# One activation function for the second MoE's gate, named ring places, and another order of the work

## The chip, the cores and the metric

The kernel runs on one core of a Trainium2 chip. The metric is the device time of one execution in microseconds (us). The core has a matrix engine (TensorE, PE in the profile; its weight loads are PEld), three elementwise engines (VectorE is DVE, ScalarE is ACT, GpSimd is POOL) and a queue that issues DMA transfers (SyncE, SP). Each engine runs its own instructions in the order written, and waits on semaphores for the others.

## The reference

Attention of 4 batches and 8 heads (576 positions, 64 wide) with a threshold, then two MoE layers over the 2304 tokens it gives (512 wide, hidden 2048), all in fp32:

```python
scores = scale * q @ k.T
scores = where(scores >= max(scores) - tau, scores, -1e9)
attn = exp(scores - max(scores)); attn = attn / (sum(attn) + 1e-9)
x = (attn @ v)                       # heads side by side: 2304 x 512
h = x @ w1_in;  x = (h * clip(h + 3, 0, 6) / 6) @ w1_out
h = x @ w2_in;  x = (h * 1 / (1 + exp(-1.702 * h))) @ w2_out
```

## The kernel before, in words

**Precision.** An fp32 operand of a matmul is split into a high part and the low remainder, and each product is three matmuls (high by high, high by low, low by high). A split is a copy on ScalarE (the high part) and a subtraction on VectorE or GpSimd (the low part, `tt`, L494, so all of these stand under L495). Weights arrive in another number format and are decoded by two ScalarE, three VectorE and one GpSimd instruction each (`decode`, L521, tile `wmstg`), then split into rings of eight tiles (`inhring`, `inlring`, `outhring`, `outlring`).

**Stages.** From 0 to about 408 us the 16 pairs of heads are attended to (`unit`, L637): scores into the two `ps` banks of PSUM, a row maximum (L764), a threshold (L765), the exponential on ScalarE (L767), mask and sum (L768), normalising (L783 or L791), transposes by TensorE that are copied out of PSUM (`et`, L837 or L838), and the product with v (L910, L926). TensorE also does the first half of the first MoE in that time (`moe_a`, `gated`, L988 and L1013). To about 650 us the rest of the first MoE follows (`moe_b`, `wide`, L1103). From 650 us the second MoE runs in ten passes (`moe2`, L1252): two halves of the hidden width, each over four blocks of 512 tokens and one of 256. Half of its weights are decoded as these passes begin, kept in DRAM and fetched again.

**The second MoE's inner step.** `hidden2` (L1201) makes two hidden tiles from seven products in place of eight. Its partial sums go through ScalarE copies (`p`, `u`) and VectorE sums (`c`). `gate2` (L1188) then makes from each `c` the two operands `g` (high and low) of the output matmuls:

```python
add(ACT, ..., "RL",  activation(out=t, in_=c, func=Sigmoid, scale=1.702))   # L1195, tile tc
add(DVE, ..., "GT2", t = t * c)                                             # L1196, under L495
add(ACT, ..., "GH",  gh = copy(t))                                          # under L492
add(eng, ..., "GL",  gl = t - gh)                                           # under L495, eng POOL or DVE
```

There are 80 calls: 64 of 512 columns and 16 of 256. The output matmuls of a step (L1013, tile `py`) come after the hidden products of the next (L1214, tile `pm`).

**Places of tiles.** `buf` (L444) names a ring of tiles; all tiles of a ring share one tag of the pool, and the pool hands out the place that was given back first. In `Plan.link` (L184) the planner orders a tile's first use after all uses of the tiles one to two rings back.

**Order of the work.** Nothing is left to the framework: the functions above only add operations with a cost and a due time to a plan. `Plan.settle` (L337) takes two tables that stand in the file: `SWAPS`, the numbers of operations that run on their other engine (for instance a low part on VectorE rather than GpSimd), and `RANKS`, one priority for each of the 6046 operations. `Plan.order` (L212) then fills the engines by those priorities with modelled costs, keeping VectorE's and GpSimd's operations named in `PORT` from overlapping and at most eight transfers in flight. `Plan.fill` (L352) puts small matmuls on zeros and ones (L1379) where the plan leaves TensorE empty. The instructions are written in the order that comes out.

Of the kernel before, what the change touches and what calls it, by code (L numbers as in the profile page):

```python
# [1437 lines left out]
```

## Time and profile before

| | |
|---|---|
| time, median of 3 runs | 1052.87 us (1051.63 to 1053.76) |
| the profiled execution's own time | 1053.79 us |
| its span, first to last instruction | 1052.0 us |
| granted TensorE clock, mean | 0.999 |
| TensorE busy | 1032.8 us, 98% of the span |
| VectorE busy | 784.3 us, 75% |
| ScalarE busy | 609.6 us, 58% |
| GpSimd busy | 447.0 us, 42% |
| DMA | 150.09 MB, 143 GB/s in the mean |

The busy time of an engine is the union of its instructions. TensorE's instructions overlap: a matmul is shown from its entry to its modelled end, and the next one starts before that. So the pace of a run of matmuls is read from the time of the run over its count, and the idle time shown for TensorE is a little less than what a wait costs.

### The profile page before, as it was taken

Reading aid. Unit: us, or ns where it says so; the run is one execution under the profiler, and the core shown is the slowest. Engines: PE = TensorE matmul, PEld = TensorE weight load, DVE = VectorE, ACT = ScalarE, POOL = GpSimd, SP = SyncE. Lnnn points to the kernel's source line nnn. Section 1 sums busy time; section 2 is a strip of 40 time slices with the busy share of each in tenths; the row PEclk is TensorE's granted clock in tenths of the full one; section 3 lists DMA queues with packets and bytes.
Section 4 is the critical chain, followed back from the end, with each engine's and each line's share of the span. In section 5 each row is a group of like instructions: output and inputs, shape, how many; then the busy total and the mean of one; then the engine's idle time right before and its main releaser. Section 6 shows DMA issues by size and latency. Waiting matters only on the chain.

```text
span 1052.0 us, 19278 instructions
## 1 busy us (share of the span) xinstructions
PE 1032.8 (98%) x6962; PEld 931.5 (89%) x6962; DVE 784.3 (75%) x1642; ACT 609.6 (58%) x1208; POOL 447.0 (42%) x555
## 2 busy tenths in 40 slices
PE   8999899999999999999999999999999999999998
PEld 6677788798979888999999999899888988998988
DVE  7999899998989884778783356888787686465543
ACT  5897776666767775646443225665655565354433
POOL 5578778765867642555440116322331231000000
PEclk9999999999999999999999999999999999999999
DMA  8434465776867565346642314346463452321201
GB/s 228 123 107 139 138 184 170 200 196 185 244 205 199 179 200 158 110 147 210 208 139 78 95 56 138 104 149 195 136 203 108 145 173 59 101 81 41 88 33 51
DMA packets 86527, 150.09 MB, mean 143 GB/s; under 512 B 8480, under 2 KB 48032, under 8 KB 84384
## 3 DMA queue, kind: packets, MB, share of 16 engines
q1 hardware_dynamic: 86288, 148.57, 47.2%
q8 instruction: 55, 0.90, 0.4%
q14 instruction: 40, 0.33, 0.1%
q10 hardware_dynamic: 144, 0.29, 0.1%
HBM read 101.52 MB, written 47.32 MB: 141 GB/s over the span
## 4 chain that ended last, share of the span: by engine, by line
PE 81%; DVE 8%; ACT 3%; POOL 3%; issue 2%; DMA 2%; SPq 0%; DVEq 0%; ACTq 0%; POOLq 0%
PE py L1013 24%; PE pm L1214 14%; PE pm L988 10%; PE pm L1013 9%; PE pm L1103 7%; PE ps L708 5%; PE pm L926 4%; PE pm L834 4%; PE ps L748 1%; DVE g L495 1%; PE pm L910 1%; PE ps L732 1%; DVE outlring L495 1%; DMA wrawstg<-kept 1%; DVE e L768 1%
## 5 line engine op out<-in xcount | busy, mean ns | idle before, releaser
L1013 PE MATMUL py<-g,outhring 128*128 128x512 f32 (+3 forms) x1024 | 280.6, 358 | 2.4 <-DVE g L495 2.1
L1013 PEld LDWEIGHTS py<-g,outhring 128*128 128x128 f32 x1024 | 179.0, 188 | 21.0 <-DVE g L495 3.5
L1013 PE MATMUL py<-g,outlring 128*128 128x512 f32 (+3 forms) x512 | 182.8, 357 | 0.0
L1214 PE MATMUL pm<-outhring,inhring 128*128 128x256 f32 x512 | 145.0, 283 | 0.9 <-ACT u L492 0.4
L1214 PE MATMUL pm<-outlring,inhring 128*128 128x256 f32 x512 | 144.2, 282 | 0.9 <-DVE outlring L495 0.9
L1214 PE MATMUL pm<-outhring,inlring 128*128 128x256 f32 x512 | 143.8, 281 | 0.0
L764 DVE TENSOR_REDUCE nm<-ps 128x1 f32<-128x576 f32 x144 | 106.3, 750 | 15.6 <-PE ps L708 12.2
L767 ACT ACTIVATE e<-ps,nm 128x576 f32<-128x576 f32 x128 | 93.4, 739 | 38.9 <-DVE nm L764 33.4
L495 POOL TENSOR_TENSOR wmstg<-wmstg,wrstg 128x512 uint32<-128x512 uint32 x48 | 67.9, 1415 | 109.7 <-DVE wmstg L548 74.3
L495 POOL TENSOR_TENSOR g<-tc,g 128x512 fp32r<-128x512 f32 x24 | 33.2, 1384 | 185.1 <-ACT g L492 154.2
L768 DVE SCALAR_TENSOR_TENSOR e<-ps,th,e 128x576 f32<-128x576 f32 x128 | 102.7, 810 | 8.0 <-ACT e L767 6.0
L1013 PE MATMUL pm<-g,outhring 128*128 128x256 f32 (+1 forms) x512 | 106.5, 299 | 0.0
L495 POOL TENSOR_TENSOR g<-t,g 128x256 fp32r<-128x256 f32 (+2 forms) x68 | 61.4, 905 | 105.8 <-ACT g L492 91.0
L1013 PEld LDWEIGHTS py<-g,outlring 128*128 128x128 f32 x512 | 96.3, 188 | 11.1
L1214 PEld LDWEIGHTS pm<-outhring,inhring 128*128 128x128 f32 x512 | 96.6, 189 | 6.1 <-ACT u L492 1.6
L1214 PEld LDWEIGHTS pm<-outlring,inhring 128*128 128x128 f32 x512 | 96.8, 189 | 4.7 <-DVE outlring L495 1.6
L1214 PEld LDWEIGHTS pm<-outhring,inlring 128*128 128x128 f32 x512 | 97.3, 190 | 0.0
L988 PE MATMUL pm<-xh,inhring 128*128 128x256 f32 (+1 forms) x320 | 96.9, 303 | 0.2
L988 PE MATMUL pm<-xh,inlring 128*128 128x256 f32 (+1 forms) x320 | 94.5, 295 | 0.0
L988 PE MATMUL pm<-xl,inhring 128*128 128x256 f32 (+1 forms) x320 | 94.4, 295 | 0.0
L708 PE MATMUL ps<-kqv 128*128 128x288 f32 x480 | 81.5, 302 | 3.2 <-DVE e L768 1.5
L1013 PEld LDWEIGHTS pm<-g,outhring 128*128 128x128 f32 x512 | 82.3, 189 | 1.7 <-issue 1.4
(147 smaller groups left out, 2426.5 us busy)
## 6 DMA issues: line engine op xcount, KB each, us to landing
turned<-tr SPq DMA_DIRECT2D x16, 1024.0 KB, 3.9
et<-turned SPq DMA_DIRECT2D x64, 256.0 KB, 5.6
wrawstg<-in_w1i_dram SPq DMA_DIRECT2D x16, 512.0 KB, 4.0
wrawstg<-in_w1o_dram SPq DMA_DIRECT2D x16, 512.0 KB, 3.8
wrawstg<-in_w2i_dram SPq DMA_DIRECT2D x16, 512.0 KB, 4.0
wrawstg<-in_w2o_dram SPq DMA_DIRECT2D x16, 512.0 KB, 3.8
qk<-in_k_dram SPq DMA_DIRECT2D x24, 288.0 KB, 3.9
qk<-in_q_dram SPq DMA_DIRECT2D x24, 288.0 KB, 4.7
```

The source lines that it names most:

```text
L495: return lambda: (nc.vector if eng == DVE else nc.gpsimd).tensor_tensor(out=o(), in0=a(), in1=b(), op=op)
L708: nc.tensor.matmul(ps.t[:, i, :SH], q, w[hd].t[:, i * SH:(i + 1) * SH], start=a, stop=z)
L732: nc.tensor.matmul(ps.t[:, i, :SH], f32(qzb.t)[:, q0:q0 + P], f32(khb.t)[:, i * SH:(i + 1) * SH], start=True, stop=True)
L764: add(DVE, 672, K("R", s), "R", lambda: nc.vector.tensor_reduce(out=nm.t[:, c], in_=ps.t[:, :, :SH], op=ALU.max, axis=AX.XY, negate=True), ...
L767: add(ACT, 624, K("X", s), "X", lambda: nc.scalar.activation(out=ev(), in_=ps.t[:, :, :SH], func=ACTF.Exp, bias=nm.t[:, c]), [ps, (nm, s)] ...
L768: add(DVE, 736, K("M", s), "M", lambda: nc.vector.scalar_tensor_tensor(out=ev(), in0=ps.t[:, :, :SH], scalar=th.t[:, c], in1=ev(), op0=ALU ...
L834: nc.tensor.transpose(pt.t[:kn, o:o + P], src(), id_b.t)
L926: nc.tensor.matmul(pv[p].t[64 * hd:64 * hd + 64, :CH[p][1]], v_(k, hd), et_m(p, turned)[:, hd, k], start=k == 0, stop=False)
L988: nc.tensor.matmul(ph.t[:, :n], a, v, start=(cc == 0 and i == 0), stop=(cc == KC - 1 and i == 2))
L1013: nc.tensor.matmul(py.t[:, :n], a, v, start=(st and i == 0), stop=(sp and i == 2))
L1103: nc.tensor.matmul(ph.t[:, :n], a, v, start=(cc == 0 and q == 0), stop=(cc == KC - 1 and q == 2))
L1214: nc.tensor.matmul(o.t[:, :n], u.t[:, ws], v.t[:, xv], start=(st and kk == 0 and i == 0), stop=(sp and kk == 1 and i == 2), skip_group_che ...
```

## The change

Four things differ. `gate2` has one ScalarE instruction where it had a ScalarE and a VectorE instruction, so there are 80 operations fewer and all later operations have lower numbers. `buf` gives each place of a ring a tag of its own, so that a tile's place is its number modulo the ring's length. `RANKS` is another table (5966 numbers). `SWAPS` is another table: 294 entries in place of 291, of which 183 name the same operation as before.

```diff
 RANKS = """
-3IGWJhXH{B2mnO@LI55D)B$G!K>}?7@d20uivf`VkO5i&$N_x;bODY5<pGod!U1>zk^!IrxdG$>7XtSISOMt)vH_+6!2xptase&^#Q`h=90IHX^Z~U2(gFDa+yR6Em;pHg)&cqfqXFRo4g$sj?g97#u>m3iVglm<?Ey*xRs#M38v?Qdr2%vT
...
 SWAPS = (
-    22, 72, 185, 192, 212, 235, 236, 264, 269, 288, 309, 331, 340, 350, 360, 371, 393, 398, 486, 528, 542, 597, 630, 657, 659, 737, 738, 746, 803, 814, 846, 874, 880, 890, 892, 929,
...
+    22, 72, 113, 192, 212, 236, 247, 264, 269, 288, 309, 321, 331, 336, 340, 360, 371, 393, 486, 528, 542, 551, 597, 630, 657, 659, 667, 697, 713, 717, 719, 745, 814, 846, 874, 880,
...
@@ -442,7 +441,9 @@
     def buf(tag, ring, pool, shape, dt=F32):
-        return Buf(pl, tag, ring, lambda: pools[pool].tile(shape, dt, tag=tag, name=tag, bufs=ring), pool)
+        b = Buf(pl, tag, ring, None, pool)
+        b.make = lambda: pools[pool].tile(shape, dt, tag=f"{tag}{b.idx % ring}" if ring > 1 else tag, name=tag, bufs=1)
+        return b
@@ -1192,8 +1193,7 @@
-        add(ACT, act(T), K("RL2"), "RL", lambda: nc.scalar.activation(out=v(t)(), in_=v(c)(), func=ACTF.Sigmoid, scale=1.702), [c], [t])
-        add(DVE, dve(T), K("GT2"), "GT2", tt(DVE, v(t), v(t), v(c), ALU.mult), [c], [t])
+        add(ACT, act(T), K("RL2"), "RL", lambda: nc.scalar.activation(out=v(t)(), in_=v(c)(), func=ACTF.Gelu_apprx_sigmoid), [c], [t])
         add(ACT, 42 + act(T), K("GH2"), "GH", copy(v(gh), v(t)), [t], [gh])
```

The entries of `SWAPS`, counted with the operations they name: TensorE's copies `et` (L837) go to VectorE 23 times (18 before), remainders of the probabilities (`pk`, L783) 33 times (26 before), first-MoE high parts and remainders 13 and 23 times (15 and 27 before), the high parts of the first MoE's input (`xh`, L941) 4 times (11 before); the thresholds (L765) go to ScalarE 57 times (51 before). The number of VectorE operations in the plan goes from 1498 to 1405.

## Rows read from the trace of the kernel before

**Rows 1.** The page's first part: busy time, share of the span, instructions.

```profile
PE 1032.8 (98%) x6962; PEld 931.5 (89%) x6962; DVE 784.3 (75%) x1642; ACT 609.6 (58%) x1208; POOL 447.0 (42%) x555
```

**Rows 2.** Windows by stage: stretch, its length, engines' busy us, clock, DMA.

```profile
0.00:12.00 12.00, 9.83 (x45) 8.40 (x46) 6.54 (x20) 3.29 (x4) 5.71 (x24) 1.00 0.68 194
12.00:130.00 118.00, 111.83 (x791) 87.53 (x790) 111.25 (x265) 98.36 (x191) 82.94 (x103) 1.00 0.48 141
130.00:408.00 278.00, 274.54 (x2102) 240.95 (x2101) 243.54 (x587) 188.92 (x383) 180.89 (x295) 1.00 0.67 191
408.00:650.00 242.00, 241.62 (x1478) 235.23 (x1477) 156.98 (x301) 110.88 (x203) 95.47 (x77) 1.00 0.44 135
650.00:790.00 140.00, 136.64 (x898) 125.04 (x897) 113.09 (x200) 85.69 (x175) 45.46 (x32) 1.00 0.51 161
790.00:920.00 130.00, 129.75 (x820) 117.03 (x819) 87.61 (x155) 68.08 (x139) 27.48 (x19) 1.00 0.37 116
920.00:1052.00 132.00, 128.56 (x843) 117.31 (x841) 65.25 (x119) 54.38 (x116) 9.06 (x7) 1.00 0.18 59
```

**Rows 3.** The chain that ended last, its end: start us, us, what.

```profile
1039.82 9.00 PE py L1013 x75
...
1048.85 0.42 DVE yc L495
```

**Rows 4.** Waits of TensorE, 650 to 1052 us: total us, times, longest; longest two.

```profile
PE py L1013 <- DVE g L495: 1.8, 3, 0.9
PE pm L1214 <- DVE outlring L495: 0.9, 2, 0.7
```

**Rows 5.** Timeline around one such wait: start us, us, instruction, idle before.

```profile
710.50 0.42 DVE L495 TENSOR_TENSOR tc<-tc,c 128x256 f32<-128x256 f32 x1
710.84 1.50 DVE L495 TENSOR_TENSOR g<-tc,g 128x256 fp32r<-128x256 f32 x1
712.60 0.41 DVE L495 TENSOR_TENSOR g<-tc,g 128x256 fp32r<-128x256 f32 x1
...
710.72 1.34 POOL L495 TENSOR_TENSOR wmstg<-wmstg,wrstg 128x512 uint32<-128x512 uint32 x1 [16.56 <-ACT g L492]
...
712.40 0.38 PE L1013 MATMUL py<-g,outhring 128*128 128x256 f32 x1 [0.94 <-DVE g L495]
```

**Rows 6.** Groups of instructions, 650 to 1052 us: the gate's four, and L545.

```profile
L495 DVE TENSOR_TENSOR tc<-tc,c 128x512 f32<-128x512 f32 (+1 forms) x80 | 54.7, 686 | 26.2 <-ACT tc L1195 25.2
L1195 ACT ACTIVATE tc<-c 128x512 f32<-128x512 f32 (+1 forms) x80 | 46.8, 588 | 29.6 <-DVE c L495 26.2 <-DVE g L495 1.1 <-POOL g L495 1.1
L492 ACT ACTIVATE g<-tc 128x512 fp32r<-128x512 f32 (+1 forms) x80 | 46.4, 587 | 40.0 <-DVE tc L495 32.4 <-PE py L1013 7.4
L495 DVE TENSOR_TENSOR g<-tc,g 128x512 fp32r<-128x512 f32 (+1 forms) x56 | 39.9, 721 | 14.0 <-ACT g L492 11.2 <-PE py L1013 2.3
L545 ACT ACTIVATE wmstg<-wrawstg 128x512 f32<-128x512 f32 x18 | 11.9, 667 | 5.8 <-DMA kept<-wmstg 3.7 <-DVE wmstg L546 0.9 <-DVE inlring L495 0.6
```

**Rows 7.** Table loads of ScalarE among the groups of the whole span.

```profile
L767 ACT ACT_TABLE_LOAD x1 | 1.3, 1283 | 1.2 <-PEq L1426 1.2
L1195 ACT ACT_TABLE_LOAD x1 | 1.3, 1283 | 0.0
```

**Rows 8.** Waits of TensorE, 12 to 408 us: total us, times, longest.

```profile
PE pm L834 <- ACT et L837: 2.1, 5, 0.7
PE ps L708 <- DVE e L768: 1.5, 2, 0.8
PE pm L834 <- POOL er L783: 1.4, 1, 1.4
PE ps L708 <- DVE kqv L495: 1.1, 1, 1.1
```

**Rows 9.** Two groups of VectorE's instructions over the span.

```profile
L768 DVE SCALAR_TENSOR_TENSOR e<-ps,th,e 128x576 f32<-128x576 f32 x128 | 102.7, 810 | 8.0 <-ACT e L767 6.0 <-ACT th L766 0.3
L838 DVE COPY et<-pm 128x512 f32<-128x512 f32 (+1 forms) x18 | 10.9, 620 | 3.9 <-PE pm L834 2.7 <-DMA et<-turned 1.1
```

More of the change, by code (lines that the diff above doesn't have):

```diff
@@ L119 @@
[L119 to L120 removed]
+3IGWJ&H*g~2LMC>LjbG-9|E@lb^^NrQ38_!$pOj%?*W_v*8#=>+X1Qpn*z-N4g#nF;Q_1x?g3l^CIVvulL7Yu^8xY!1_HqWxdC7T9s;fcjRN}t6awu5AOZ>k>H)n0&jHc``~f%u=m8=EMFJ2400K<{GXgmRaso60YXV0CW&%V4X#!9J2LiVO
@@ new lines @@
+3j)~zuL6t$UILT?oC4Sa2m|#3Rsu)@=>nMo?*a(|5(An7ZURyQ+yd$X1OmhY&jMWn^a5uBR044Vr~=&rkpjO0^8#uDk^)ZxN&*D}3<HJ&Hv*~xC<C$rP6LAiWdipC;sP!M_5lq7egd)qzX7}fumO?*mjdGfKLb?*#R69XWCHO4p#h=+n*n42
+g8_>HjscGWP5}-9+5oWt*#NEpbOS~MqXQ!Y%>p+A<^p5`s{?5PN&zwfzycou-T=@5qyTpSQUERh4FHD%3jhQF6#>Ely#S^F6aWtZ004>rMgq105(1q9CjzDc3<4Pf-vI#t5&$It2ml2DApl|kRRFXALI45)5db^@3;+fI8~~{Rwg9yNUjQZm
+8Uic;%mS7Gr2(A)Fak{gcmlHkRRW0t{{f`}>j7;6%mFI`VFK&{?E+%~;{rzkQ~_@Ri2_IgIssMzF999_)dJ}Obpk#DB?2h|Dgu83F9HJqKLD%%Bmfft9{^hbl>n0fGXM|(Bmpr2{s8O%BLGVQ@BnH7=>Wa}odL@L7y?WI4+2>Me*w1uNdhhb
@@ new lines @@
+<O0|MIs&i)u>!gQdjcT>3IqB9KmytUbONIR9Rf@Od;-$}7Xq^ZngN~xsRGCXfdZcbhy!c_xB?Xd;sIj-(E#`W^#G0ltpGg%T>+>7b^w<E@c<eD8v(xnSpfS0WdXqevH(E=JOU5_76L*6{Q*A#HUbX;Jp%0jtOHsCz5!VRf&yLv0Rq$nYXran
+f&tV4+XB)7E&}HPo&o{_(E<4Z<pKTyfCAwHa{?g)h67sy6$5ty69Rz%i~!F7;{a~}c>ucrI01tINC0dAi2&CC*Z^w)C;*fIrvPdIGysnPBLbfQZUIFAlLLSNVF7*spaER~W&pSW2m-VL!vWy{PypWpwgf={DF7Y-iUD5%cmYcSSOQ`K%K`}j
+(*O$rDgm|vG6M?(D+3n;-~qY<ivltN`~p1#IRnQ6R09G7iUK+VA_EZvQUh574+AU%l>%A=Yy$uT8UsE9l>-<9Ujr=zGXuN>XagAo9Rqv=>jLBh&I4})mje?6M*~Fztpnl%WdoE0g9ESw=mIkY$pWGPJ^*V07yxz-bqa0@{sa93s0054D*?Iy
@@ new lines @@
+wE=Me-3mMl`3ma;vI8&#IRpU#>HsqVSq1P4#R~cgk^traV*||t@&g+LSOjbY5DQxh!3s(MjR4yK#{g*nIRJA2`~Y+SPXKiQhX95EH~=63Z~@Q(sR1nk1Oui53<dB3%K>i!H3IMgmjR>#F#;R|)d4~RECB-pQ322bg#rNsy8=oBGy_Bf4FlN%
+6az^Ecmv)7fCB^p{{XQ8?f~Eb#sCumc>zQL7XcChrvWqpB>|oQnE>km@&I@MnE}WFg#mH_b^#~?fB~lhBmz4EZ~|xoeF3uq#R1U*-2v_b`vM*V-vW{YU<29$&I0%W{Q|xN5(L)*2?I<3O8`3oQ2;#vF#ucu4FN^~Hvn1y5dmlbIsh902mxXN
+pa7)+dI2y2SOM<<PXV_BfdMK5^a1_?PyucONdc(?!vb6bUjhyTB?EH<K?6twAOn2^X9J)Dm;&kqUIbSIn*-<o)Bv9W)d0W%kN^q+`2fTL<NyN!^Z;7}<p5y-uK>6Jxd1x=ssLvJs{oh)!~nSi$N-`P9076#BLQLs3<10Xb^~Gq0|Z_JCjlG;
@@ new lines @@
+{{kumoddH2ngiAW!~@?1?gZ!qqyzT=A^}?g+yNs5$OGX6It11ODFnL%K?Jk|F9Zw(r37#Ungk&PyaZYV(FAG)p9B^J`2z3*O9XlZ*#t@iLj<q{cm!hvtpuS2cLccveFWJCqy$I=b_B!(f&@tfvIMaOaRiA3TLh{E1_kH@`UFG@U<9lL2nF~A
+g#_mW;{;&@zyn_d0R%P$!UVqro&*RB9SZ3R7X`HhKm`^BLIp$x$OJV74GT029t$xAI|V8Qcm>J@p9Pr(NClA#6$`!!Y6Xr3T?L2*(gl76rUlsrk_-F_QwwGT5dygakOHj&UIp<2@&d{NQvxpo`T_<6Z321%1q0^-s{$zl-~yoneFz!^asYk<
+H3Pi@uK^|j>;kj`j{;Kxa0BH7jsvj+4FuN%DFOHb76WJn9RY{{7y(=Xz5><&Km*DH+XL+bbpz=G-2>VKwgVUh2n50d3IrwuWdsxiSOXUX5(SV1g#da0eE@p^Dgc}SumIfv+yGPnG62N~#RJp=Z3E8(%mV@hf&*Ox!vjGAHUPc`c?5a``U5Zn
@@ L121 @@
++ZI3<C>Qn?M;8Yd;T8}VAr~7L85aZ>&lV~d;}#JY1{V$&#})w>`xeF)LKiI;_ZImU2^YN<I2Se-!xlpq?G`Z?GZ)wvN*6U3?iM2#AQwLu(H0mNFc&@-9v2!H)D}w@wiYxOI~V8{4;MujdluXl=@udv3KvNi
 """
 SWAPS = (
[10 rows of a table removed]
[10 rows of a table added]
 )
```

153 lines of the change are left out of this document (69 added, 84 removed), and 18 rows, old and new, of the table SWAPS.

## The prediction

> **What bounds the kernel now.** I read the page's busy times first, then the windows by stage, then TensorE's waits, and last the timeline around single waits. TensorE is busy for 1032.8 of 1052.0 us and no other engine for more than 784.3 [rows 1]. The windows [rows 2] show where it isn't: the difference of a stage's length and its PE busy time is 2.17 us at the start, 6.17 from 12 to 130 us, 3.46 to 408, 0.38 to 650, 3.36 to 790, 0.25 to 920 and 3.44 to the end, 19.23 in all. The clock column is 1.00 in every stage, so nothing is to be won there. The last matmuls run to 1048.82 and the last VectorE sum starts at 1048.85 [rows 3]; about 3.2 us of the 3.44 are that tail of sum and store, which the change leaves as it is. So about 14 us of idle time lie between start and tail, and no edit that leaves the matmuls alone can be worth much more. A little more, since idle time understates a wait: the last 75 matmuls pass at 9.00 / 75 = 0.12 us each [rows 3], but the one after a wait is shown for 0.38 us [rows 5]; about 0.2 us of an emptied pipe goes with each wait.
>
> The change touches the second MoE by its edit and the rest by its order alone, so the sum has one term for each.
>
> **The gate.** It removes 80 VectorE products of 0.686 us, 54.7 us in all [rows 6], a fifth of VectorE's 113.09 + 87.61 + 65.25 = 265.95 us in this stage [rows 2]. ScalarE keeps its 80 instructions of 0.588 us. The new function is in no row; its nearest rows are the copy of the same shape, 0.587 us, and another function at 0.667 us on wholly 512-wide tiles [rows 6], where the gate's mean holds 16 narrow ones. So it costs between nothing and 80 x 0.08 = 6.4 us of ScalarE, on an engine that is busy 208 of 402 us there [rows 2]; I take nothing, by the copy. Below nothing is excluded, as the copy does less and takes as long.
>
> Most of the 54.7 us was off the path. What was on it is seen in the waits: TensorE waited 1.8 us for the low parts `g` and 0.9 for the remainders `outlring` [rows 4], all of both made by VectorE. The timeline shows why they were late [rows 5]: a `g` of 256 columns that takes 0.41 us at its next place took 1.50, from 710.84, beside a GpSimd sum on weights from 710.72 for 1.34 us. TensorE's 0.94 us of idle time ends with it. So the waits come from VectorE and GpSimd being held up by one another in a moment that the order did not foresee. A product of the gate, 0.42 us, stood right ahead of it on VectorE, from 710.50 [rows 5]; without it the low part can start some 0.4 us sooner (0.69 where the tiles are 512 wide), before the GpSimd sum rather than behind it. What stays is the collision itself, with the roles changed.
>
> The Trainium skill, "SBUF — State Buffer", section on the two separate sides, says that a VectorE instruction with two SBUF inputs and a GpSimd instruction that reads SBUF exclude each other for a whole instruction, and whichever starts first holds the other up. The stretched `g` agrees: 1.34 us of GpSimd and then its own work. By that rule alone, with the moments of collision left to chance, taking out a fifth of VectorE's work there would take a fifth of these waits, some 0.7 us.
>
> I price the term from the idle time of 650 to 1048.8 us: 3.36 + 0.25 + (3.44 - 3.2) = 3.85, and about 8 waits with 0.2 us more each, 1.6; together 5.4 us are at stake. The lower end is all of it, -5.4. The upper end is that the same waits return once more behind other instructions, +3.8. I take -3.0: the 3.36 us of the first window, where VectorE is at 81% and where 0.4 to 0.7 us are taken from ahead of each late instruction, less a tenth. What would be late next is the partial sum `c` ahead of ScalarE, which waited 26.2 us for it already [rows 6]; it has slack, for TensorE has the products of the next step to do meanwhile.
>
> **The wait that is gone.** ScalarE sat idle for 40.0 us before the high parts, 32.4 of them until the product was there [rows 6]; afterwards two ScalarE instructions follow one another. Behind the new function on ScalarE stand the copies `p` and `u` out of PSUM, on which TensorE's next products hang. They move up, not back, as ScalarE has no longer to wait for VectorE between. I cost it at nothing beyond the term above; if the copies came later by one function, that is 0.588 us on one step, hidden by the other matmuls of the step, of which six alone last 0.7 us at 0.12 each.
>
> **Named places.** No instruction is added. A tile now waits for the tile one ring back and not for the place given back first. Rows of the nearest wait: the copy into `g` waited 7.4 us for TensorE to be done with a place [rows 6]. So it bounds the cost at +3 us, if half of that came onto the path, and at -1, if the pool's choice had been the worse one in the waits above. I take nothing, since the plan that makes the order already holds each tile back until the whole older ring is done. Transfers follow the same rule, and behind a held load on SP's queue would stand the loads of the next pass; the two longest waits of TensorE in this stage are none of that queue's [rows 4].
>
> **The order before 650 us.** Here instructions change places and engines, none goes. VectorE is at 111.25 of 118 us from 12 to 130 and 243.54 of 278 to 408 [rows 2], so the waits are those of a nearly full engine: 1.5 us for the masked probabilities, 2.1 for `et` from ScalarE, and single waits of 1.4 and 1.1 [rows 8]. `SWAPS` moves five more copies `et` (0.620 us each [rows 9]) and seven more remainders onto VectorE, and six thresholds, seven high parts and some weight parts away from it; my count leaves VectorE's load there the same within 1 us. So only the order can win or lose. The idle time at stake is 6.17 + 3.46 + 0.38 = 10.0 us, the lower end is half of it, -5, because the waits are ten or more of different kinds and a new order keeps some; the upper end is +7.3 (the second rival). I take -1.0: the two long single waits (1.4 and 1.1) are accidents of one place that another order does not repeat, and short ones replace them in part.
>
> **The sum.** -3.0 for the gate, -1.0 for the order, 0 for the rest: -4.0 against the profiled execution's 1053.79 (its span of 1052.0 and 1.8 around it). That execution was 0.92 us above the median of 1052.87; against the median the sum is 1048.9, which I state as 1049.0.
>
> **The rivals.**
>
> Nothing measurable (0.23). The collisions in the second MoE are those of weight work on GpSimd, which stays, and by the skill's rule above only a fifth of the waits goes. Then the gate wins about 0.7 us, the order nothing: 1052. For it: the sum is a quarter of one per cent of a kernel at 98% of TensorE. Against: the late low part stood right behind a product in VectorE's queue.
>
> Slower (0.16). Copies `et` move onto the engine that is already 94% busy from 12 to 130 us. There each of eight half units has a copy, 0.620 us, that can come in ahead of a mask and sum of 0.810 us, on which a score tile's place in PSUM hangs [rows 9]. Each mask that is late costs 0.81 us on TensorE. Four such (3.2 us) eat the gate's gain; from seven on (5.7 - 3.0 = 2.7) the kernel is measurably slower; nine give 7.3 - 3.0 = +4.3, 1057. For it: waits of this kind are there already, two of 0.8 at most [rows 8]. Against: six thresholds leave VectorE.
>
> A larger gain (0.15). The new order also takes half of the waits before 650 us: -5.4 - 5.0 = -10.4, 1042.5. For it: ten unlike waits, none of which is needed by the data alone. Against: a full VectorE.
>
> Table loads (0.03). If the copies and weight functions needed another table than the new function, ScalarE would load one at each change. Two loads of 1283 ns are all that the trace has, at the first exponential and at the first gate [rows 7]; the copies, and the function of L545, run on both sides of the second with no third. With one of them missing beside the new function, 80 gates need up to 160 loads, 205 us on an engine with 194 us to spare: 1100 or more. The skill's page "ScalarE: Activation LUTs", section on table sets, says that the cheap functions are in every set; hence so low a chance.
>
> **How the numbers follow.** My forecast, 1046 to 1050.7, has 0.43. What a measurement can tell from no change is 0.2%, 2.1 us: faster is below 1050.8, slower above 1055.0. Faster is 0.43 + 0.15 = 0.58, the same 0.23, slower 0.16 + 0.03 = 0.19. For 8 in 10 the range goes from the larger gain's 1042.5 to 1056.5 on the slower side, just short of its nine late masks.
>
> **What would show it.** After the change, VectorE's busy time should fall by some 55 us and ScalarE's stay within 7. PE's idle time from 650 to 790 us should fall from 3.36 to about 1; a stretched `g` beside a GpSimd weight sum should still be found, with no idle TensorE behind it. Idle time from 12 to 408 us should stay between 5 and 10. I am wrong if the second MoE's idle time stays above 3, if the first 408 us change by more than 5 either way, or if a third table load is there.

## The result, and the profile after

The changed kernel takes 1043.18 us in the median of four runs (1042.77 to 1043.67), the kernel before 1052.25 in the same comparison: 9.1 us less, ratio 0.9913 [0.9895, 0.993]. The forecast was 1049.0, with 1046 to 1050.7 as its own range and 1042.5 to 1056.5 for 8 in 10. The direction was right and the size was not: the time lies below the first range and just inside the second, where the prediction had put its rival of a larger gain, 1042.5.

The first part of the page of the changed kernel answers to [rows 1]; its columns are the same.

```profile
PE 1027.4 (99%) x6956; PEld 930.7 (89%) x6956; DVE 732.9 (70%) x1549; ACT 612.1 (59%) x1220; POOL 448.5 (43%) x556
```

VectorE is busy for 51.4 us less, ScalarE for 2.5 more. TensorE has six matmuls fewer, all of them fills (below), and 5.4 us less busy time. The windows of the changed kernel, cut as in [rows 2]:

```profile
0.00:12.00 12.00, 9.83 (x44) 8.39 (x45) 6.49 (x20) 3.25 (x4) 5.79 (x24) 1.00 0.69 206
12.00:130.00 118.00, 112.72 (x810) 90.33 (x809) 112.89 (x268) 99.55 (x195) 85.79 (x107) 1.00 0.47 144
130.00:408.00 278.00, 275.98 (x2116) 242.73 (x2115) 243.89 (x587) 190.07 (x390) 182.40 (x292) 1.00 0.69 195
408.00:650.00 242.00, 241.92 (x1466) 235.70 (x1466) 155.84 (x293) 111.17 (x206) 94.27 (x77) 1.00 0.43 131
650.00:790.00 140.00, 139.22 (x927) 127.57 (x926) 99.52 (x181) 88.61 (x183) 44.73 (x32) 1.00 0.52 167
790.00:920.00 130.00, 130.00 (x830) 117.85 (x829) 71.17 (x124) 71.03 (x144) 27.77 (x21) 1.00 0.33 105
920.00:1040.90 120.90, 117.75 (x775) 108.15 (x773) 43.14 (x81) 48.40 (x103) 7.74 (x6) 1.00 0.20 64
```

Length less PE busy: TensorE's idle time from 650 to 790 us is 0.78 (3.36 before), from 790 to 920 none, from 12 to 130 us 5.28 (6.17), to 408 us 2.02 (3.46). The clock is 1.00 throughout.

Windows of a fixed time hold different work in the two kernels, so I cut both at the same work: where 3571 matmuls have passed that are not fills (all but three of them are the same in both). Fills are the small matmuls that `fill` puts into gaps; there are 58 before and 52 after, all ahead of the cut. The two windows of the kernel before:

```profile
0.00:501.06 501.06, 488.88 (x3629) 428.90 (x3630) 432.31 (x1008) 345.48 (x684) 322.81 (x464) 1.00 0.60 175
501.06:1052.00 550.94, 543.90 (x3335) 502.61 (x3333) 351.95 (x634) 264.12 (x525) 124.20 (x92) 1.00 0.36 113
```

and of the changed kernel:

```profile
0.00:495.70 495.70, 486.15 (x3623) 428.80 (x3624) 432.09 (x1000) 346.63 (x694) 324.24 (x462) 1.00 0.61 177
495.70:1040.90 545.20, 541.27 (x3335) 501.92 (x3333) 300.85 (x549) 265.45 (x527) 124.24 (x95) 1.00 0.36 114
```

So the change won 5.4 us in the first part, where no instruction of the gate is, and 5.7 in the second, which holds the whole second MoE. In the second part the idle time falls from 7.04 to 3.93 us, and the busy time of 3335 matmuls in each from 543.90 to 541.27. I read the latter as restarts of an emptied pipe, which idle time doesn't show; the run of the gate alone, below, bears this out.

TensorE's waits in the second MoE of the changed kernel, as in [rows 4]; the view has this one row:

```profile
PE py L1014 <- POOL g L496: 0.7, 1, 0.7
```

The gate's groups there, as in [rows 6], and the table loads, as in [rows 7]:

```profile
L1196 ACT ACTIVATE tc<-c 128x512 f32<-128x512 f32 (+1 forms) x80 | 46.7, 587 | 31.2 <-DVE c L496 28.6 <-DVE g L496 1.1 <-POOL g L496 0.7
L493 ACT ACTIVATE g<-tc 128x512 fp32r<-128x512 f32 (+1 forms) x80 | 46.6, 585 | 14.1 <-PE py L1014 12.6
L496 DVE TENSOR_TENSOR g<-tc,g 128x512 fp32r<-128x512 f32 (+1 forms) x56 | 37.4, 670 | 54.2 <-ACT g L493 53.8
...
L768 ACT ACT_TABLE_LOAD x1 | 1.3, 1283 | 1.2 <-PEq L1426 1.2
L1196 ACT ACT_TABLE_LOAD x1 | 1.3, 1283 | 0.0
```

The new function takes 587 ns, the sigmoid took 588, and there is no third load. The Trainium skill, "ScalarE: Activation LUTs", section "What ACT_TABLE_LOAD costs", says that every function has the same cost per element; by that row the trace agrees. ScalarE no longer waits 32.4 us for VectorE ahead of the high part. VectorE now waits for ScalarE ahead of the low part, 53.8 us where it was 11.2: it has room, and what comes late is no longer in its queue.

A stretched low part is still there, as the prediction asked. The timeline of the changed kernel at 852 us:

```profile
851.97 1.70 DVE L496 TENSOR_TENSOR g<-tc,g 128x512 fp32r<-128x512 f32 x1 [0.21 <-ACT g L493]
...
851.83 2.99 POOL L496 TENSOR_TENSOR inlring<-wrawstg,inhring 128x512 fp32r<-128x512 f32 x2 [1.30 <-DVE inhring L562]
```

The low part takes 1.70 us beside a GpSimd remainder of the weights, and TensorE is not idle for a moment from 790 to 920 us.

The one wait left in this stage is at the first gate:

```profile
661.33 1.28 ACT L1196 ACT_TABLE_LOAD   x1
662.63 0.63 ACT L1196 ACTIVATE tc<-c 128x512 f32<-128x512 f32 x1
...
664.13 1.28 POOL L496 TENSOR_TENSOR g<-tc,g 128x512 fp32r<-128x512 f32 x1 [13.14 <-ACT g L493]
...
665.46 0.50 PE L1014 MATMUL py<-g,outhring 128*128 128x512 f32 x1 [0.68 <-POOL g L496]
```

The table load stands ahead of the first gate on ScalarE, the low part follows on GpSimd, and TensorE waits 0.68 us for it.

TensorE's waits from 12 to 408 us in the changed kernel, the longest rows, as in [rows 8]:

```profile
PE pm L835 <- DVE et L839: 1.1, 1, 1.1
PE ps L709 <- DVE e L769: 0.9, 2, 0.6
PE pm L835 <- ACT et L838: 0.9, 2, 0.7
PE ps L733 <- DMA g<-in_q_dram: 0.8, 1, 0.8
...
PE ps L709 <- DVE kqv L496: 0.6, 1, 0.6
```

The 1.4 us behind GpSimd's `er` are gone, and the waits for ScalarE's `et` fell from 2.1 to 0.9, with a new one of 1.1 for VectorE's.

### The profile page after: what moved, and what is told of

It reads as the page before. It is cut to its first block, busy times and chain, and to the rows that moved or that the text cites. A ratio compares the mean times of both kernels' runs of the same rounds, so it can differ in the third digit from the quotient of the medians.

```text
span 1040.9 us, 19211 instructions
## 1 busy us (share of the span) xinstructions
PE 1027.4 (99%) x6956; PEld 930.7 (89%) x6956; DVE 732.9 (70%) x1549; ACT 612.1 (59%) x1220; POOL 448.5 (43%) x556
## 4 chain that ended last, share of the span: by engine, by line
PE 91%; DVE 4%; DMA 1%; ACT 1%; issue 1%; POOL 1%; SPq 0%; ACTq 0%; DVEq 0%
PE py L1014 28%; PE pm L1214 16%; PE pm L989 11%; PE pm L1014 9%; PE pm L1104 7%; PE ps L709 6%; PE pm L927 5%; PE pm L835 4%; PE pm L911 2%; PE ps L749 1%; PE ps L733 1%; DVE nm L765 1%; PE pm L931 1%; DVE e L769 1%; DMA wrawstg<-in_w1i_dram 1%
## 5 line engine op out<-in xcount | busy, mean ns | idle before, releaser
L765 DVE TENSOR_REDUCE nm<-ps 128x1 f32<-128x576 f32 x144 | 106.3, 750 | 12.5 <-PE ps L709 7.3
L496 POOL TENSOR_TENSOR g<-t,g 128x256 fp32r<-128x256 f32 (+2 forms) x71 | 64.1, 907 | 100.5 <-ACT g L493 76.9
L1014 PEld LDWEIGHTS py<-g,outlring 128*128 128x128 f32 x512 | 96.2, 188 | 11.2
```

Source lines behind the costliest of these rows:

```text
L496: return lambda: (nc.vector if eng == DVE else nc.gpsimd).tensor_tensor(out=o(), in0=a(), in1=b(), op=op)
L765: add(DVE, 672, K("R", s), "R", lambda: nc.vector.tensor_reduce(out=nm.t[:, c], in_=ps.t[:, :, :SH], op=ALU.max, axis=AX.XY, negate=True), ...
L1014: nc.tensor.matmul(py.t[:, :n], a, v, start=(st and i == 0), stop=(sp and i == 2))
```

## The experiments

An edit is made to the kernel before ("old order") or to the changed one ("new order"); it is shown cut to what matters, and `...` stands for what is left out. The kernel before was run beside each and took 1052.2 to 1052.6 us in the median; ratios are against it. Differences to the changed kernel are against the 1043.18 above.

**The new gate alone.** The old order keeps its place for the product, but nothing is issued there.

```diff
-  act(T) ... func=ACTF.Sigmoid, scale=1.702
-  dve(T) ... tt(DVE, v(t), v(t), v(c), ALU.mult)
+  act(T) ... func=ACTF.Gelu_apprx_sigmoid
+  dve(T) ... lambda: None
```

> The kernel before with the new gate function alone: the 80 VectorE products are gone, every other instruction stands in the order of before, tiles share their places as before. Theory ORDER (the gain of 9.1 us comes from the order; the gate is a small part): between 1049.5 and 1051.5, PE idle time from 650 us on falls by 1 to 2 us, the first 408 us unchanged. Theory GATE (the second MoE's whole 5 to 6 us are the products that no longer stand ahead of the late low parts): 1046 to 1047.5, PE idle time from 650 to 790 us falls from 3.36 to about 1.

Measured: 1049.26 us (1048.18 to 1050.99), 0.9972 [0.9961, 0.9983]: between the two, nearer ORDER. By parts it reads otherwise:

```profile
0.00:503.07 503.07, 489.56 (x3629) 429.63 (x3630) 432.45 (x1008) 345.92 (x684) 323.87 (x464) 1.00 0.60 174
503.07:1049.10 546.03, 541.83 (x3335) 502.65 (x3333) 308.32 (x554) 262.96 (x525) 119.63 (x92) 1.00 0.37 114
```

The second part is 4.9 us shorter than before, 2.8 of it idle time and 2.1 busy time of the same matmuls. Both kernels pass them in the same order, so the two traces can be compared one matmul at a time: 4.6 of the 4.9 us, among them 1.7 of the 2.1, lie within eight matmuls of the ten places where TensorE is idle in one of them. So this busy time, too, belongs to the waits. The first part, in which nothing was edited, is 2.0 longer. Of TensorE's waits in the second MoE those for `g` are gone, and only this is left, as it was:

```profile
PE pm L1214 <- DVE outlring L495: 0.9, 2, 0.7
```

**What happened in the first part.** VectorE waits there for one load, of a `qk` tile for the attention. The timeline of the kernel before, and of the gate alone:

```profile
215.35 0.52 DVE L682 TENSOR_SCALAR qk<-qk,sc 128x576 f32<-128x576 f32 x1 [1.42 <-DMA qk<-in_q_dram]
```

```profile
216.32 0.52 DVE L682 TENSOR_SCALAR qk<-qk,sc 128x576 f32<-128x576 f32 x1 [2.34 <-DMA qk<-in_q_dram]
```

TensorE's wait for GpSimd's `er` is 1.4 us in the one [rows 8] and 2.3 in the other, as long as VectorE's. The chain of waits of the kernel before, just ahead of that:

```profile
208.91 1.42 POOL kqv L495
210.33 0.02 issue
210.34 4.88 DMA qk<-in_q_dram
```

The load goes out right when an instruction of GpSimd ends, and its 4.88 us are on the chain. From issue to landing (the last column, us) this load takes, in the kernel before, in the gate alone, and in two kernels from further down in which nothing waits for it, named places alone and no fills:

```profile
qk<-in_q_dram SPq DMA_DIRECT2D x1, 288.0 KB, 4.9
qk<-in_q_dram SPq DMA_DIRECT2D x1, 288.0 KB, 5.8
qk<-in_q_dram SPq DMA_DIRECT2D x1, 288.0 KB, 3.1
qk<-in_q_dram SPq DMA_DIRECT2D x1, 288.0 KB, 2.9
```

In all four it goes out between 209.7 and 210.4 us. What differs is how long it is under way, and where that is long it stands at the head of VectorE's queue.

In the gate alone something follows that the kernel before doesn't have. Three windows of it:

```profile
213.00:216.80 3.80, 3.80 (x32) 3.62 (x30) 1.46 (x5) 0.57 (x2) 0.39 (x2) 1.00 0.76 176
216.80:219.20 2.40, 0.08 (x2) 0.06 (x2) 2.40 (x9) 2.24 (x5) 2.10 (x5) 1.00 1.08 215
219.30:222.60 3.30, 3.30 (x17) 3.30 (x17) 2.96 (x7) 3.25 (x9) 3.14 (x4) 0.50 0.57 130
```

TensorE stands idle for 2.3 us and is then granted a clock of 0.50, the lower of its two levels (1.2 GHz), at which 17 matmuls pass in 3.30 us, where 32 passed in 3.80 ahead of the wait. At the pace ahead of the wait 17 take 2.0 us, so I estimate the cost of the clock at 1.3 us. With the 0.9 us by which the wait is longer it is the size of the 2.0 by which the first part is longer, and neither is seen to come from the gate, whose instructions stand behind 650 us. In the kernel before, the granted clock after its wait of 1.4 us is 1.00. So the first part of these two kernels is a poor base for a difference of 2 us.

**Named places alone**, in the old order.

```diff
-  pools[pool].tile(..., tag=tag, name=tag, bufs=ring)
+  pools[pool].tile(..., tag=f"{tag}{b.idx % ring}", name=tag, bufs=1)
```

> The kernel before with named ring places alone, the same instructions in the same order on every engine. Theory PLACES (a part of the waits were for a place that the pool chose badly): at least 1.5 us faster than before. Otherwise 1051.5 to 1053, no change that can be measured.

Measured: 1051.30, 0.9986 [0.9977, 0.9995]: PLACES failed; 0.9 us is barely clear of nothing. In this kernel's profile nothing waits for the load:

```profile
0.00:499.02 499.02, 488.65 (x3629) 429.20 (x3630) 433.48 (x1008) 345.88 (x684) 323.71 (x464) 1.00 0.60 175
499.02:1049.30 550.28, 543.61 (x3335) 502.46 (x3333) 350.81 (x634) 263.84 (x525) 124.66 (x92) 1.00 0.37 114
```

**The new order with the old gate.** Sigmoid again, and VectorE's product put ahead of each high part; all other instructions keep the new order.

```diff
-  act(T) ... func=ACTF.Gelu_apprx_sigmoid
+  act(T) ... func=ACTF.Sigmoid, scale=1.702
+  def high():
+      tt(DVE, v(t), v(t), v(c), ALU.mult)()
+      copy(v(gh), v(t))()
...
```

> The changed kernel with the old gate put back into the new order: sigmoid on ScalarE, and the product on VectorE just ahead of each high part; 80 products that the order has no room for, all other instructions in the order of the changed kernel. Theory ORDER: the new order carries 80 x 0.686 us of unplanned VectorE work with at most 2 us of loss, 1043.5 to 1045.2. Theory GATE: the second MoE loses what it won, 1048 to 1049.5.

Measured: 1068.09, 1.0149 [1.0135, 1.0163], 24.9 us above the changed kernel. Both theories missed it by more than 18 us. All of it is in the second part (the first is 495.79):

```profile
495.79:1065.80 570.01, 552.99 (x3335) 500.91 (x3333) 355.30 (x629) 265.15 (x527) 125.48 (x95) 1.00 0.35 109
```

ScalarE's longest row of waits and TensorE's two longest in this kernel's second MoE:

```profile
ACT g L493 <- DVE tc L496: 58.9, 67, 2.3
```

```profile
PE py L1014 <- DVE g L496: 2.8, 8, 0.6
PE py L1014 <- ACT yc L493: 2.1, 1, 2.1
```

ScalarE waits 67 times for a product that its order didn't reckon with, and the delay reaches TensorE through many rows, none of them long.

**The new order with the old choice of places**, the edit of the places undone.

> The changed kernel with the pool choosing the places again. Theory PLACES: at least 1.5 us slower than the changed kernel, 1044.7 or more. Otherwise 1042.5 to 1044, no difference.

Measured: 1042.43, 0.9903 [0.9887, 0.9918], as the changed kernel. In the new order the places are worth nothing that can be seen. In the old order they come with 0.9 us and with no wait for the load; that they took the wait away isn't shown, since the run without fills, below, has no such wait either and still has the old choice of places.

**The product twice**, in the old order.

```diff
-  tt(DVE, v(t), v(t), v(c), ALU.mult)
+  lambda: [tt(DVE, v(t), v(t), v(c), ALU.mult)() for _ in range(2)]
```

> The kernel before with the gate's product done twice on VectorE, the second right behind the first, so the gate computed is h times h times the sigmoid: the same 80 unplanned products in the chain to the high part as the changed kernel bore with the old gate (25 us more), but in the order of before. Theory SLACK (the new order of the second MoE leaves more room between a step's parts): the old order loses clearly more, 1084 us or over. Theory FIT (each order is tight around the durations it was made for, the old no more than the new): the loss is the same within 5 us, 1072 to 1082.

Measured: 1093.24, 1.0383 [1.0365, 1.0401]: 40.7 us more, SLACK's number. TensorE's longest row of waits in its second MoE:

```profile
PE py L1013 <- DVE g L495: 11.1, 15, 2.2
```

80 more products are some 55 us of VectorE, and about 70% of that came onto the path: the old order had no room for them, though VectorE was busy for only 64% of the stretch (351.95 of 550.94). A small part is TensorE's clock. In the profiled execution 0.52 and 0.51 were granted in two stretches of the second part, from 721.6 to 725.1 and from 806.9 to 810.4 us, behind waits for `g` of 1.71 and 2.21 us. The one execution with a mean granted clock of 1.000 took 1091.13, 38.5 us more. SLACK's number is reached, but not its reason: VectorE does 160 products here (busy 411.45 us of the second part) and 80 in the run that it was to be compared with (355.30), so the two losses don't compare the room in the two orders.

**The product beside the chain**, in the new order: it is done, but onto a tile that nobody reads any more, so that the high part doesn't wait for it.

```diff
+      tt(DVE, v(c), v(t), v(c), ALU.mult)()
       copy(v(gh), v(t))()
...
```

> The changed kernel with its new gate and, at the place where the old gate's product stood in the last but one experiment, a VectorE product of the same two tiles that writes onto c, which nobody reads any more: the same 80 products with the same wait for ScalarE, but nothing in the gate's chain waits for them. Theory CHAIN (the 25 us are the product's latency between ScalarE's two instructions): at most 6 us slower than the changed kernel, below 1049. Theory LOAD (they are VectorE's time, and the wait for ScalarE in front of what is queued behind): 1058 to 1068.

Measured: 1053.22, 1.0007 [0.9998, 1.0017]: 10.0 us above the changed kernel, between the two expectations. A row of VectorE's waits in the second MoE that the changed kernel doesn't have:

```profile
DVE c L496 <- ACT tc L1196: 30.8, 30, 6.2
```

So of the 24.9 us of the new order with the old gate, 10 are VectorE's time and its wait for ScalarE in a queue that wasn't planned for them, and 15 come with the wait on the way to the high part.

**Small delays in both orders.** Every fourth row maximum of the attention has one more small VectorE instruction behind it, 32 in all.

```diff
+  if s % 4 == 1:
+      nc.vector.tensor_scalar(out=nm.t[:, c], in0=nm.t[:, c], scalar1=1.0, scalar2=1.0, ...)
```

> The kernel before with a small VectorE instruction of about 0.2 us (the row maximum times one) behind each fourth row maximum of the attention, 32 in all, 6.5 us that the order has no room for. Theory SLACK: the old order loses 5 us or more in the first 408 us, 1057 or over, and at least twice what the new order loses by the same. Theory FIT: both orders lose the same within 1.5 us.

> The changed kernel with the same 32 small VectorE instructions in the attention. Theory SLACK: at most 2.5 us slower than the changed kernel, 1045.7 or less. Theory FIT: the same loss as in the old order within 1.5 us, some 5 us, 1048.

Measured: old order 1055.62, 1.0032 [1.0021, 1.0042], 3.0 us more than without; new order 1045.19, 0.9927 [0.9911, 0.9944], 2.0 more. By the first parts of the profiles (table below) it is 504.58 against 501.06, 3.5 us, and 498.48 against 495.70, 2.8. SLACK's 5 us in the old order did not come, and the profiles don't show twice the loss. FIT's equal loss within 1.5 us holds, but not its size of some 5. By the ratios the new order loses 1.5 us and the old 3.4, with intervals of 1 to 2 us on each, so a small difference isn't excluded.

**Four q and k places in the old order**, beside the named ones, so that the late load can start earlier.

```diff
+  more = {"qk": 4}.get(tag, ring)
...
```

> The kernel before with named places and a fourth place for the attention's q and k loads, every instruction in the order of before. In the traces of the old order VectorE waits 0 to 2.3 us for one q load at 210 us that is issued only when its place comes free, and TensorE behind it for 0 to 2.3 us. Theory LATE LOAD (this is where about 2 of the old order's 5.4 us in the first 500 us go): that wait is gone in the trace, 3571 matmuls are done by 499.2 us or sooner, and the time is 1050 to 1051. Theory ELSEWHERE: the wait is gone but the stage ends no sooner than 500.5 us, and the time is 1051.3 or more.

Measured: 1051.23, 0.9989 [0.9978, 1.0]. VectorE's wait for the load is gone: the load goes out at 208.26 us, two us sooner, and is under way for 4.8 us as in the kernel before. But the named places alone show no wait either, and take as long. So the fourth place isn't seen to be worth anything.

**No fills after 12 us**, in the old order.

```diff
-  if count > 0:
+  if count > 0 and s < 12000:
```

> The kernel before without the filling matmuls on zeros and ones after the first 12 us (some 30 matmuls of 0.11 us, 3.3 us of TensorE), the rest in the order of before. Theory FILLS (the fills stand where a late input has already used up the room, so they delay what follows): 1.5 us or more faster, 1050.8 or less. Theory COVER (they lie in time in which TensorE would wait anyway): no change, 1051.8 to 1053; a lower granted clock would show in the first 230 us if they were needed for it.

Measured: 1050.32, 0.9978 [0.9969, 0.9987], the number of FILLS. But its two windows don't bear out the reason:

```profile
0.00:498.87 498.87, 485.33 (x3604) 425.24 (x3604) 432.23 (x1008) 345.50 (x684) 323.42 (x464) 1.00 0.60 175
498.87:1048.60 549.73, 543.13 (x3335) 502.42 (x3333) 350.93 (x634) 263.69 (x525) 124.21 (x92) 1.00 0.36 114
```

With 26 fills fewer TensorE's busy time in the first part is 3.3 us below that of the named places alone (488.65), but its idle time is 3.2 above (13.54 against 10.37): TensorE stood idle where it had filled. The part is 0.15 us shorter. This kernel, too, has no wait for the late load, and by the profiles that is the 2 us against the kernel before. So what the fills cost by themselves is not shown; by these windows it is next to nothing.

**More places in the new order**, four for `qk` and three for the gate's `tc`.

> The changed kernel with a fourth place for the q and k loads and a third for the second MoE's gate tile tc, the same order. If waits for places still cost anything in the new order: 0.5 us or more faster than the changed kernel, 1042.6 or less. If not: the same within 0.5 us.

Measured: 1042.93, 0.9907 [0.9893, 0.992], no different from the changed kernel.

**All three in the old order:** the new gate, four q and k places, no fills after 12 us.

> The kernel before with all that can be had without another order: the new gate function, named places with the fourth place for q and k loads, and no fills after 12 us. If the terms add up: the gate's 3.0, the late load's 1 to 2 and the fills' 0 to 2, so 1046 to 1048.5; what is then left to the changed kernel's 1043.2 (3 to 5 us) is the order's alone.

Measured: 1046.52 (1046.11 to 1046.99), 0.9942 [0.993, 0.9955], as expected. The changed kernel is 3.3 us below it: what its order is worth beyond all of these, by the medians.

**The parts side by side.** Each kernel was cut at the same 3571 matmuls; us, worked out from two windows of each profile:

| kernel | first part | second part |
|---|---|---|
| before | 501.06 | 550.94 |
| new gate alone | 503.07 | 546.03 |
| named places alone | 499.02 | 550.28 |
| four q and k places | 499.26 | 550.54 |
| few fills | 498.87 | 549.73 |
| all three, old order | 498.75 | 546.05 |
| product twice | 503.01 | 590.19 |
| old order, delays | 504.58 | 549.52 |
| after | 495.70 | 545.20 |
| new order, old places | 495.94 | 545.26 |
| new order, more places | 495.51 | 544.89 |
| new order, delays | 498.48 | 545.02 |
| new order, product beside | 496.25 | 555.25 |
| new order, old gate | 495.79 | 570.01 |

The table orders what the medians blur. Each row is one execution. Old order and old gate: 550.4 in the mean of four second parts (549.73 to 550.94). With the new gate in the old order 546.03 and 546.05: the gate is worth 4.3 us (3.7 to 4.9). In the new order 545.1 (three kernels): the order adds 0.9 there, in size the wait for `outlring`, which is 0.9 with the new gate alone and gone in the new order. In the first part the old order takes 499.0 in the mean of the four kernels without the wait for the late load, and 501 to 503 in the three with it and no delays (the two at 503, gate alone and product twice, have the stretch of lower clock behind the wait); the new order takes 495.7 (three kernels): 3.3 less, or 5.4 less than the profiled execution before. The sum is 4.3 + 0.9 + 3.3 = 8.5. The medians differ by 9.1; the 0.6 left is in size a part of the late load, which costs about 2 us where the profiles show it, but its share in the unprofiled runs is not seen. Their spread points the same way: the times of named places and of no fills lie within 1.1 us (11 runs each), those of the kernel before within 3.2 to 5.3 us (17 to 21 runs). The four q and k places, with 2.7, don't fit so well.

The median of the gate alone puts the gate at 3.0 (1.8 to 4.1 by its interval) and leaves 6 to the order. The medians of the last two old-order kernels, few fills and all three, which differ by the gate and by the fourth place, put it at 3.8.

## Why the prediction was right, and where its sizes were off

**The gate: right as far as the traces show, -3.0 was -4.3 by the second parts (-3.0 and -3.8 by medians).** The prediction's reason was that the product stood in VectorE's queue right ahead of low parts that came late. The kernel before shows it at its second-longest wait for such a part (0.64 us) as at the longest of [rows 5]:

```profile
782.93 0.68 DVE L495 TENSOR_TENSOR tc<-tc,c 128x512 f32<-128x512 f32 x1
783.15 1.62 POOL L495 TENSOR_TENSOR wmstg<-wmstg,wrstg 128x512 uint32<-128x512 uint32 x1 [3.01 <-ACT g L492]
783.53 1.78 DVE L495 TENSOR_TENSOR g<-tc,g 128x512 fp32r<-128x512 f32 x1
```

At the third, of 0.22 us, a remainder of the weights stands ahead, and no product. With the new gate alone the waits for `g` are gone from TensorE's rows, and the idle time from 650 to 790 us is 140.00 - 138.99 = 1.01, in the old order still. But that edit takes away two things, the product's time in VectorE's queue and ScalarE's wait for it ahead of the high part. Which of them freed the low parts in the old order was not tried; in the new order the wait costs more than the time (15 us against 10). The 0.9 us for `outlring`, which the prediction counted with them, stayed until the order changed. The step that was mis-sized is "I take -3.0: the 3.36 us of the first window ... less a tenth". The lines ahead of it had put 0.2 us of emptied pipe to each wait, 1.6 in all, and the value taken left them out. The second part shows them: 2.1 us of the 4.9 in the run of the gate alone are busy time of the same matmuls. The measured term lies about midway between the value taken and its bound of -5.4.

**The collisions stay, with no wait of TensorE behind the one shown.** The prediction said that a fifth of the waits would go if collisions alone made them. Every wait for `g` in VectorE's hands went, while a low part of 1.70 us is still there. The Trainium skill, "SBUF — State Buffer", in the section on the two separate sides, has the two engines hold each other up; by that row the trace agrees. But the waits weren't in proportion to the collisions. I take it that the room ahead of TensorE's need counted; no run changes that room alone.

**ScalarE's function and the wait that is gone: 0 and 0, both right as prices.** 587 against 588 ns, and the copies out of PSUM did not become a wait of TensorE. The prediction gave the wait no price beyond the gate's term, since what stands behind it moves up. The runs show that its price hangs on the order, which the prediction didn't ask: in the new order the wait is worth 15 us and the product beside it 10 (the two runs with a VectorE product), while in the old order, which was made with both, taking both away gained 4.3.

**Named places: 0, about right.** 0.9986 [0.9977, 0.9995] in the old order, 0.9 us by the medians and inside the term's bounds of -1 and +3, and no difference in the new.

**The order before 650 us: -1.0 was about -3.3, and -5.4 against the profiled execution.** This is the step that failed by most. The prediction let the two long single waits go and short ones replace them in part. The 1.4 went (it was the late load), and the 1.1 for `kqv` went to 0.6. It counted idle time and single waits; the gain lies in many places. Read at the same matmul, the changed kernel is ahead of the one with named places by 2.0 us at 118 us, 3.0 at 270 and 3.3 at the cut. At equal work the new order has 0.8 us less idle time than the old one with named places, 9.55 against 10.37, and 2.5 less TensorE busy time, 486.15 against 488.65. Six fills fewer explain some 0.8 of that (26 fewer were 3.3); the rest is matmuls of the same work, passed closer together. Why this order does it is not settled. The two delayed runs don't show that it bears delays better, and it isn't the places. Which part is the table of `RANKS` and which that of `SWAPS` was not tried.

**The rivals.** The one of a larger gain came nearest: it had -5.4 for the gate and -5.0 for the order, against 4.3 and 4.2 by the parts. The slower one did not come. VectorE has 23 copies `et` of 648 ns in place of 18, and from 12 to 130 us it is a little fuller than before, 112.89 against 111.25 of 118 us; the masks `e` made TensorE wait 0.9 us, less than the 1.5 of [rows 8], and one copy 1.1. No third table load came either.

**The signs.** VectorE's busy time fell by 51.4 us (some 55 foretold); ScalarE's rose by 2.5 (within 7); the idle time from 650 to 790 us is 0.78 (about 1) and from 12 to 408 us 7.30 (5 to 10). One mark of error was nearly reached, a change of over 5 us in the first 408. The windows, of the kernel before and of the changed one:

```profile
0.00:412.60 412.60, 400.80 (x2972) 341.49 (x2973) 363.19 (x874) 293.30 (x583) 270.28 (x422) 1.00 0.62 178
```

```profile
0.00:408.00 408.00, 398.53 (x2966) 341.45 (x2967) 363.27 (x872) 292.87 (x587) 273.97 (x421) 1.00 0.63 180
```

Less 58 and 52 fills these are the same 2914 matmuls, 4.6 us apart.

## What to carry to other kernels

Price a wait of the bounding engine by the time in which the same instructions pass, not by idle time alone: here 2.1 of 4.9 us were restarts inside "busy". Cut both profiles at equal work before you split a difference of a few us among edits; the median put the gate at 3.0 where the second parts show 4.3, and in the profiled execution an unedited stretch had moved by 2, most of it, by the estimate above, in a stretch of lower clock. Look at the granted clock in short windows, not in the mean: 0.998 over that run is 0.50 over some 3 us. An order written out by hand fits the instructions that it was made for: one taken away from it gave 4.3 us, the same one put into an order made without it cost 24.9, so what an instruction costs has to be asked of each order anew.

## What the runs showed of the hardware

- 80 VectorE products of 0.69 us, 55 us in all, cost between 10 and some 40 us of the run with VectorE busy for less than three quarters of the stretch (355.73 of 555.25 us with the product beside the chain). Free time of an in-order queue in the mean isn't free time where it is needed.
- Without the fills after 12 us the granted clock of TensorE stayed at 1.00 in both windows: no run here shows that they were needed for it.
- TensorE's granted clock fell to its lower level in the middle of two of these kernels: in the new gate alone after TensorE had stood idle for 2.3 us (0.50 from 219.3 to 222.6 us), and in the product twice at three places, the first after the same wait, 1.8 us there. After the wait of 1.4 us in the kernel before it stayed at 1.00.
- One DMA load of 288 KB was under way for 2.9 to 5.8 us in kernels that issue it at the same point of the order. It held up VectorE by 1.4, 1.8 or 2.3 us in three kernels with the same instructions up to there, and not at all in others that differ in places or fills. What sets its time was not found.
